# The last four blocks of wo in strips of columns, eight of the strips as two loads of unequal rows

## Chip, cores and metric

The kernel runs on one core of one Trainium2 chip. The metric is the device time of one execution in microseconds (us). Three runs of the kernel before took 773.12 to 773.62 us, median 773.36.

## What is computed

One decode step for a batch of 2 with D = 1024. Branch a is attention over a cache of 32,768 positions (32 query heads, 4 heads of keys and values, head size 128, all fp32); branch b is a small mixer with two layer norms, of which two weights (w1, w2) are not needed at sequence length 1, since every shift by one or two positions leaves only zeros. A sigmoid gate mixes the two:

```python
g = sigmoid((x * gate_w).sum(-1, keepdims=True))
q = (x @ wq)                              # per head
p = softmax(q @ k.T * Dh ** -0.5)
a = concat(p @ v) @ wo                    # wo: 4096 x 1024
b = x + gelu(layernorm(x) @ w3) @ w4      # hs is zero at S = 1
out = g * a + (1 - g) * b
```

The caches and weights are 331 MB, and each byte is used once.

## The kernel before, in words

**Storage.** Two large buffers (`ring`, tiles load0 and load1, 64 KB per partition each) take everything that streams in: wq, w3, the keys and values of eight pairs of batch and head, w4 in between, and most of wo. A third buffer, `tail` (4 * D columns, line 137), is used once, for the last four of the 32 blocks of wo. A block is 128 rows by 1024 columns.

**Order of the transfers.** All big loads are issued by SP through `load` (line 217), in program order, each as soon as the buffer that it writes is free: SP waits for TensorE's mark and then issues. Each load adds 16 to a semaphore once it has fully landed. At the end of the stream wo comes in three pieces into the ring (`weights(wo, STEPS, ...)`, line 272, with 14, 9 and 5 blocks), then four loads into `tail` (lines 273 to 275): blocks 0 and 1 as one load of 128 rows by 2048 columns, then blocks 2 and 3 as 1280, 512 and 256 columns. These four wait for nothing, as `tail` is written only once. They are the last loads of the program; behind them on SP is only the store of `out` (line 640), which has 8 rows.

**What waits for them.** The table `came` (line 215) names the semaphore and the count that says that each of the four has landed: got_x at 32 (16 of them from the load of xg at the start), b_in, pt_in and k1_free. TensorE waits for them at lines 621, 627, 631 and 633.

**The end on TensorE.** After the eighth pair, `weigh` (line 528) multiplies the 28 blocks of wo in the ring into the bank acc, one wait for each of the three pieces (L371 in the profile). Then `block(0..3)` multiplies the four blocks in `tail` into the bank final (L380): blocks 0 and 1 after came[0], then `resumed()` adds what acc holds, then block 2 and a quarter of block 3 after came[1], two quarters after came[2], the last quarter after came[3]. VectorE and ScalarE copy final to out_sb (L638), and SP stores it.

Of the kernel before, what the change touches and what calls it, by code (L numbers as in the profile page):

```python
# [14 lines left out]
P = 128  # L15
B, D, HQ, HKV, SK, DH, F = 2, 1024, 32, 4, 32768, 128, 3584
REP = HQ // HKV
PAIRS = B * HKV
# [6 lines left out]
G = P // C  # L25
# [48 lines left out]
def kernel(  # L74
# [55 lines left out]
    def new(name, *shape, parts=P):  # L130
        return nc.alloc_sbuf_tensor(name, [parts, *shape], F32).ap()
# [5 lines left out]
    tail = new("tail", 4 * D)  # L137
# [57 lines left out]
    def sem(name):  # L195
        cleared.append(nc.alloc_semaphore(name))
        return cleared[-1]
# [8 lines left out]
    got_x = sem("got_x")  # L206
# [5 lines left out]
    step, own_step, to_pe, pt_in, b_in, e_in, x_in, k1_free = (  # L212
        sem(n) for n in ("step", "own_step", "to_pe", "pt_in", "b_in", "e_in", "x_in", "k1_free"))

    came = ((got_x, 32), (b_in, 16), (pt_in, 16), (k1_free, PAIRS + 16))

    def load(dst, src, sem, *marks):
        sp.after(*marks)
        nc.sync.dma_start(dst, src).then_inc(sem, 16)

    def run(src, j):
        return src[PART * j:PART * (j + 1)].rearrange("i (q w) c -> (i q) (w c)", w=PART)
# [9 lines left out]
    def at(name, m=None):  # L232
        if m is None:
            return (pe.sem, 1 + PROLOGUE.index(name))
        return (pe.sem, len(PROLOGUE) + m * len(TURN) + m // 4 * 2 + 1 + TURN.index(name))
# [18 lines left out]
    half = PART * KF // 4  # L254
    STEPS = ((0, 14), (14, 9), (23, 5))

    def weights(src, pieces, *free):
        for (lo, n), landing in zip(pieces, w_in):
            j = lo // half
            piece = slice((lo - j * half) * D, (lo - j * half + n) * D)  # L260
            load(flat[j][:, piece], run(src, j)[:, piece], landing, free[j])
# [8 lines left out]
        for j in range(2):  # L270
            load(flat[j], run(vt[m], j), landed[j], (at("k0", m), (k1_free, m + 1))[j])
    weights(wo, STEPS, at("v0", PAIRS - 1), at("v1", PAIRS - 1))
    load(tail[:, :2 * D], run(wo, 0)[:, half * D:], came[0][0])
    for mark, lo, hi in zip(came[1:], (0, 5, 7), (5, 7, 8)):
        load(tail[:, 2 * D + lo * D // G:2 * D + hi * D // G], run(wo, 1)[:, half * D + lo * D // G:half * D + hi * D // G], mark[0])


# [37 lines left out]
    for i in range(2):  # L315
        own = slice(i * HALF, (i + 1) * HALF)
# [103 lines left out]
    for i in range(2):  # L420
        own = slice(i * HALF, (i + 1) * HALF)
        for s in range(2):
            lo = (2 * s + i) * REP
# [7 lines left out]
    for k2 in range(2):  # L431
        for g in range(G):
            lo = P * (1 - k2)
# [7 lines left out]
    n = KF // G  # L441
# [24 lines left out]
    for i in range(2):  # L466
        for j in range(2):
            own = slice(i * HALF, (i + 1) * HALF)
# [139 lines left out]
    for t, apart, lo, n in ((w_pad, C // B, 0, half), (o_last, 1, half, 2)):  # L608
        for i in range(2):
            own = slice(i * HALF, (i + 1) * HALF)  # L610
# [65 lines left out]
```

## Time and profile before

| | us |
|---|---|
| median of 3 runs | 773.36 (773.12 to 773.62) |
| span of the profiled execution | 771.6 |
| median less span | 1.8 |
| TensorE busy in the span | 436.4 (57%) |
| VectorE busy | 95.2 (12%) |
| ScalarE busy | 60.7 (8%) |
| bytes read from HBM | 331.36 MB, 429 GB/s over the span |
| SP's first issue of a load into tail | 739.90 |
| last instruction, the issue of the store of out | 770.23 |

The times inside the profile are from the start of the span; the 1.8 us between its span and the median of the runs lie outside it. PE is TensorE, PEld its loading of weights, DVE VectorE, ACT ScalarE, SP SyncE; an SPq row is the issue of a transfer and not the transfer itself. The list of DMA issues gives the size of a load and the time from its issue to its landing. In the table of windows each row is a stretch of the span, with the busy time of each engine, the clock that TensorE was granted (PEclk, 1 is full speed), the busy share of the 16 DMA engines and the GB/s that they moved. A "packet" of the DMA rows is one piece of a transfer; a transfer ends with small packets that count up its semaphore.

### The profile page before, as it was taken

What the parts mean: (1) busy time and instruction counts of PE and PEld (TensorE: products, weight loads), DVE (VectorE), ACT (ScalarE), POOL (GpSimd) and SP (SyncE); (2) the same over time, 40 slices, a digit from 0 to 9 for tenths busy, and PEclk for the clock granted to TensorE, in tenths of its full rate; (3) what the DMA queues carried; (4) which work ended last, traced back from release to release, by engine and by line L of the source; (5) the groups of instructions that cost most, each with busy time, mean ns of one, the idle gap of its engine ahead of it and who ended that gap; (6) DMA issues with size and microseconds to landing.
All of it is one profiled execution on the core that took longest, in us unless ns stands there. A gap on an engine that the chain in (4) does not pass through costs nothing. (4 is left out here: it accounts for less than half of the span.)

```text
span 771.6 us, 7439 instructions
## 1 busy us (share of the span) xinstructions
PE 436.4 (57%) x3332; PEld 199.9 (26%) x3332; DVE 95.2 (12%) x269; ACT 60.7 (8%) x144; POOL 3.8 (0%) x13
## 2 busy tenths in 40 slices
PE   0676746564645474546575446454745565646467
PEld 0232413232322232223233213121322232313134
DVE  1110202100210021002100002100210021002110
ACT  0000002000200020002000002000200020002000
POOL 1000000000000000000000000000000000000000
PEclk9977667767787768767766678777777677678788
DMA  9999999999999999999999999999999999999997
GB/s 381 435 436 436 435 436 435 436 436 431 428 431 431 435 435 435 435 435 435 430 428 440 432 435 435 435 435 435 435 435 435 431 431 435 431 435 431 431 424 327
DMA packets 6648, 331.50 MB, mean 430 GB/s; under 512 B 872, under 2 KB 1008, under 8 KB 1264
## 3 DMA queue, kind: packets, MB, share of 16 engines
q1 hardware_dynamic: 6496, 331.36, 99.4%
q8 instruction: 7, 0.11, 0.1%
q10 hardware_dynamic: 144, 0.01, 0.0%
q14 instruction: 1, 0.01, 0.0%
HBM read 331.36 MB, written 0.01 MB: 429 GB/s over the span
## 5 line engine op out<-in xcount | busy, mean ns | idle before, releaser
L488 PE MATMUL sc<-load,q_cur 128*32 128x512 f32 x1024 | 144.1, 722 | 132.3 <-PEq L53 132.3
L514 PE MATMUL pv<-load,pt 128*32 128x512 f32 x1024 | 134.2, 683 | 88.7 <-PEq L53 88.7
L488 PEld LDWEIGHTS sc<-load,q_cur 128*32 128x32 f32 x1024 | 51.2, 130 | 219.2 <-issue 214.8
L514 PEld LDWEIGHTS pv<-load,pt 128*32 128x32 f32 x1024 | 39.2, 124 | 173.9 <-issue 173.9
L505 PE MATMUL sc<-wide,p 128*128 128x128 f32 x256 | 44.5, 347 | 22.8 <-PEq L53 22.8
L571 DVE TENSOR_REDUCE mx<-sc 128x1 f32<-128x512 f32 x32 | 21.4, 689 | 284.8 <-PE sc L488 284.8
L555 ACT ACT_TABLE_LOAD x8 | 10.3, 1283 | 483.0 <-ACTq L53 483.0
L505 PEld LDWEIGHTS sc<-wide,p 128*128 128x128 f32 x256 | 40.1, 184 | 30.0 <-issue 30.0
L371 PE MATMUL acc<-load,w_pad 128*32 128x256 f32 x448 | 34.2, 478 | 18.9 <-PEq L53 18.9
L588 DVE COPY pt<-sc 64x256 f32<-64x256 f32 x64 | 25.9, 414 | 81.4 <-PE sc L505 80.9
L561 ACT COPY pt<-sc 64x256 f32<-64x256 f32 x64 | 23.5, 368 | 85.3 <-PE sc L505 83.0
L593 DVE COPY pv_sb<-pv 128x512 f32<-128x512 f32 x16 | 10.3, 686 | 145.6 <-PE tr L520 145.6
L371 PEld LDWEIGHTS acc<-load,w_pad 128*32 128x32 f32 x448 | 18.6, 137 | 33.6 <-issue 28.7
L524 PE MATMUL tr<-sel,pv_sb 128*128 128x8 f32 x128 | 18.9, 284 | 11.8 <-PEq L53 11.8
L555 ACT ACTIVATE p<-sc,bias 128x512 f32<-128x512 f32 x32 | 21.6, 686 | 0.1
L357 PE MATMUL sc<-load,x_pad 128*32 128x512 f32 x128 | 19.2, 768 | 4.1 <-PEq L53 4.1
L524 PEld LDWEIGHTS tr<-sel,pv_sb 128*128 128x128 f32 x128 | 18.4, 228 | 12.3 <-issue 12.3
L357 PE MATMUL sc<-load,xn_pad 128*32 128x384 f32 (+1 forms) x128 | 15.3, 641 | 7.9 <-PEq L53 7.9
L342 PE MATMUL tr<-xg_sb,perm 128*128 128x16 f32 x4 | 1.0, 372 | 25.2 <-DMA xg_sb<-xg 25.2
L584 DVE COPY p<-p 128x256 f32<-128x256 f32 x32 | 9.4, 294 | 26.7 <-ACT p L555 26.7
L357 PEld LDWEIGHTS sc<-load,xn_pad 128*32 128x32 f32 x128 | 4.8, 130 | 18.4 <-issue 18.4
L357 PEld LDWEIGHTS sc<-load,x_pad 128*32 128x32 f32 x128 | 4.9, 137 | 17.6 <-issue 17.5
(89 smaller groups left out, 96.3 us busy)
## 6 DMA issues: line engine op xcount, KB each, us to landing
load<-w SPq DMA_DIRECT2D x4, 7168.0 KB, 24.9
load<-wo SPq DMA_DIRECT2D x1, 7168.0 KB, 29.0
load<-wo SPq DMA_DIRECT2D x1, 4608.0 KB, 19.3
load<-wo SPq DMA_DIRECT2D x1, 2560.0 KB, 25.0
tail<-wo SPq DMA_DIRECT2D x1, 1024.0 KB, 27.0
tail<-wo SPq DMA_DIRECT2D x1, 640.0 KB, 28.1
load<-kt SPq DMA_DIRECT2D x16, 29.6
load<-vt SPq DMA_DIRECT2D x16, 29.5
```

Source lines behind the costliest of these rows:

```text
L357: last = nc.tensor.matmul(b[C * g:C * g + C, :hi - lo], pad[:, k], t[:, o + lo:o + hi], start=(k == 0), stop=(k == KD - 1))
L371: inst = nc.tensor.matmul(acc[C * g:C * g + C], lhsT, rows[:, g * (D // G):(g + 1) * (D // G)], start=False, stop=last, skip_group_check=True)
L488: last = nc.tensor.matmul(sc[i][C * g:C * g + C], q_cur[:, w, s], ring[j][:, w, o:o + 512], start=(s == 0 and w == 0), stop=(s == 1 and w ...
L505: last = nc.tensor.transpose(sc[k][:, t * P:(t + 1) * P], pair.rearrange("p w q -> p (w q)"), ident)
L514: last = nc.tensor.matmul(pv[C * g:C * g + C], pt[j][w][:, lo:lo + C], ring[j][:, w, o:o + G * DH], start=(j == 0 and w == 0 and t == 0), ...
L524: last = nc.tensor.matmul(tr[1][:, w * REP:(w + 1) * REP], pv_sb[:, s, w].rearrange("p i q -> p (i q)"), sel[:, s], start=(s == 0), stop=( ...
L555: nc.scalar.activation(p[:, i, :, :PART], sc[i].rearrange("p (t q w) -> p t w q", t=NT, w=PART), AF.Exp, bias=bias, scale=scale, accum_out ...
L561: nc.scalar.copy(*halves(1, j, c)).then_inc(pt_in, 1)
L571: last = [nc.vector.reduce_max(out=mx[:, k:k + 1], in_=sc[k], axis=AX.X) for k in ((1, 2) if i == 2 else (i,))][-1]
L584: nc.vector.tensor_copy(p[:, i, :, PART], p[:, i, :, 0]).then_inc(to_pe, 1)
L588: nc.vector.tensor_copy(*halves(0, j, c)).then_inc(pt_in, 1)
L593: last = nc.vector.tensor_copy(pv_sb[:, :, :, i], pv.rearrange("p (s q w) -> p s w q", q=HALF, w=PART))
```

## The change

The first two loads into `tail` become seventeen. Blocks 0 and 1 come as three strips of 64 columns and one of 1856 columns. Each narrow strip is two loads by the new helper `uneven`: the first n partitions, and the 128 - n others, with n = 124, 119 and 125. The first 1280 columns of blocks 2 and 3 come as five strips of 256 columns, each again two loads, with n = 120, 100, 88, 104 and 126. The last two loads (512 and 256 columns) are as before. The counts in `came` follow: got_x now goes to 16 + 7 * 16 and b_in to 10 * 16. The places of the waits, TensorE's work and every other load are the same. All line numbers behind the change move by 12.

```diff
-    came = ((got_x, 32), (b_in, 16), (pt_in, 16), (k1_free, PAIRS + 16))
+    came = ((got_x, 16 + 7 * 16), (b_in, 10 * 16), (pt_in, 16), (k1_free, PAIRS + 16))
...
     weights(wo, STEPS, at("v0", PAIRS - 1), at("v1", PAIRS - 1))
-    load(tail[:, :2 * D], run(wo, 0)[:, half * D:], came[0][0])
-    for mark, lo, hi in zip(came[1:], (0, 5, 7), (5, 7, 8)):
+    def uneven(dst, src, sem, n):
+        for own in (slice(0, n), slice(n, P)):
+            load(dst[own], src[own], sem)
+
+    narrow = 64
+    for i, n in enumerate((124, 119, 125)):
+        cols = slice(i * narrow, (i + 1) * narrow)
+        uneven(tail[:, cols], run(wo, 0)[:, half * D:][:, cols], came[0][0], n)
+    cols = slice(3 * narrow, 2 * D)
+    load(tail[:, cols], run(wo, 0)[:, half * D:][:, cols], came[0][0])
+    for i, n in enumerate((120, 100, 88, 104, 126)):
+        cols = slice(i * D // G, (i + 1) * D // G)
+        uneven(tail[:, 2 * D:][:, cols], run(wo, 1)[:, half * D:][:, cols], came[1][0], n)
+    for mark, lo, hi in zip(came[2:], (5, 7), (7, 8)):
         load(tail[:, 2 * D + lo * D // G:2 * D + hi * D // G], run(wo, 1)[:, half * D + lo * D // G:half * D + hi * D // G], mark[0])
```

On SP, the end of the program before; each row is one load with its rows and columns, first the three pieces of wo, then the four of tail and the store:

```order
L219 DMA load<-wo 128x14336
L219 DMA load<-wo 128x9216
L219 DMA load<-wo 128x5120
L219 DMA tail<-wo 128x2048
L219 DMA tail<-wo 128x1280
L219 DMA tail<-wo 128x512
L219 DMA tail<-wo 128x256
L640 DMA out<-out_sb 8x256
```

Nothing is moved past another load here. On SP in the changed program, from the third piece of wo to the second of the five strips of blocks 2 and 3:

```order
L219 DMA load<-wo 128x5120
L219 DMA tail<-wo 124x64
L219 DMA tail<-wo 4x64
L219 DMA tail<-wo 119x64
L219 DMA tail<-wo 9x64
L219 DMA tail<-wo 125x64
L219 DMA tail<-wo 3x64
L219 DMA tail<-wo 128x1856
L219 DMA tail<-wo 120x256
L219 DMA tail<-wo 8x256
L219 DMA tail<-wo 100x256
L219 DMA tail<-wo 28x256
```

The seventeen loads stand in the place of the two of 2048 and 1280 columns, behind all of the ring's loads; the loads of 512 and 256 columns and the store follow them as before.

## Prediction

> **What bounds the kernel now.** I read the page first, then the chain that ended last, then the end of the timeline, then the transfers of that end. The page says that this is a kernel of transfers:
>
> ```profile
> span 771.6 us, 7439 instructions
> PE 436.4 (57%) x3332; PEld 199.9 (26%) x3332; DVE 95.2 (12%) x269; ACT 60.7 (8%) x144; POOL 3.8 (0%) x13
> ...
> DMA  9999999999999999999999999999999999999997
> ...
> DMA packets 6648, 331.50 MB, mean 430 GB/s; under 512 B 872, under 2 KB 1008, under 8 KB 1264
> ```
>
> The 16 DMA engines are busy in every slice but the last, and TensorE is busy 57% of the time. No byte is saved by the change, so only the last slice can move. What happens there stands in the chain and in the timeline of the end:
>
> ```profile
> 758.40 0.04 issue
> 758.44 9.00 PE acc L371 x112
> 767.44 2.46 PE sc L380 x69
> ```
>
> ```profile
> 767.25 1.06 PE L380 MATMUL sc<-tail,o_wide 128*32 128x128 f32 x32
> ...
> 768.12 0.41 PE L380 MATMUL sc<-so_far,spread 128*32 128x128 f32 x8
> 768.49 0.81 PEld L380 LDWEIGHTS sc<-tail,o_wide 128*32 128x32 f32 x28 [0.23 <-DMA tail<-wo]
> 768.50 1.38 PE L380 MATMUL sc<-tail,o_wide 128*32 128x128 f32 x32
> 769.46 0.14 PEld L380 LDWEIGHTS sc<-tail,o_wide 128*32 128x32 f32 x4 [0.16 <-DMA tail<-wo]
> 769.92 0.28 DVE L638 COPY out_sb<-sc 64x128 f32<-64x128 f32 x1 [1.99 <-PE sc L380]
> 770.23 0.37 SPq L640 DMA_DIRECT2D out<-out_sb  x1
> ```
>
> From 758.44 on TensorE has work to the end. It stands still for the last four blocks of wo (tile tail) only twice, 0.23 us and 0.16 us. So the end has two limits that lie close together: the last strip of tail, and TensorE's own 11.5 us. The first, second and third piece of wo, which start TensorE at 758.44, stand ahead of the changed loads in SP's order and are not touched.
>
> The loads of tail, and the share of the DMA engines that is busy in the last microseconds (the share is the number ahead of the GB/s):
>
> ```profile
> 739.90 1.85 SPq L219 DMA_DIRECT2D tail<-wo  x4
> ...
> tail<-wo SPq DMA_DIRECT2D x1, 1024.0 KB, 27.0
> tail<-wo SPq DMA_DIRECT2D x1, 640.0 KB, 28.1
> ...
> tail<-wo SPq DMA_DIRECT2D x1, 256.0 KB, 28.3
> tail<-wo SPq DMA_DIRECT2D x1, 128.0 KB, 28.1
> ```
>
> ```profile
> 767.00:767.25 0.25, 0.25 (x11) 0.14 (x4) 0.00 (x0) 0.00 (x0) 0.00 (x0) 1.00 0.94 356
> 767.25:767.50 0.25, 0.25 (x16) 0.25 (x12) 0.00 (x0) 0.00 (x0) 0.00 (x0) 1.00 0.66 254
> 767.50:767.75 0.25, 0.25 (x20) 0.25 (x12) 0.25 (x1) 0.00 (x0) 0.00 (x0) 1.00 0.53 213
> ...
> 768.25:768.50 0.25, 0.25 (x13) 0.02 (x4) 0.00 (x0) 0.00 (x0) 0.00 (x0) 1.00 0.44 164
> 768.50:768.75 0.25, 0.25 (x14) 0.25 (x14) 0.00 (x0) 0.00 (x0) 0.00 (x0) 1.00 0.41 143
> 768.75:769.00 0.25, 0.25 (x18) 0.25 (x10) 0.00 (x0) 0.00 (x0) 0.00 (x0) 1.00 0.17 57
> ```
>
> This is the view that matters. The engines do not finish together. About half of them run dry between 767.25 and 767.5, the share then stands near one half for a whole microsecond, and the other half ends between 768.5 and 769.0. Each load is done only when its slowest engine is, so half of the engines set the end and half idle for about 1.5 us. I see a likely source in the queues between 45 and 435 us, which hold all the packets of program code in the span:
>
> ```profile
> DMA packets 2968, 169.21 MB, mean 434 GB/s; under 512 B 320, under 2 KB 320, under 8 KB 320
> ...
> q8 instruction: 7, 0.11, 0.1%
> q14 instruction: 1, 0.01, 0.0%
> ```
>
> Eight code packets (those of q8 have 16 KB each) went through the same engines, and eight engines are late. An engine that fetched code once would stay late, since its queue is never empty. Which engines these are the trace does not name.
>
> **The change part by part.** First, what a row costs an engine. The four loads were issued about 0.47 us apart from 739.90 on (1.85 us in all, the last one 0.43 of it), so they landed at 766.9, 768.5, 769.15 and 769.4. The second brings eight rows of 5 KB to each engine, and took 1.57 us, 39 ns per KB; the third, eight rows of 2 KB, 0.68 us, 42 ns per KB. I take 40 ns per KB, so 40 ns for a row of 1 KB. A row of 256 bytes is not in the trace. The nearest are the 96-byte rows of xg on the other queue:
>
> ```profile
> q10 hardware_dynamic: 48, 0.00, 0.3%
> ```
>
> In the window from 20 to 30 us, 0.3% of 16 engines over 10 us is 0.48 us for 48 packets, 10 ns each. So a 256-byte row costs at least 10 ns (which is also a quarter of 40) and at most the 40 ns of 1 KB; I take 15, near the 96-byte row and on the line between the two.
>
> [...]
>
> Second, which engine gets which rows. A transfer of 128 rows closes with one small packet per engine. The page counts 872 packets under 512 bytes, and that is 45 loads with 16 each, 144 of xg, and 8 more: the store of out, whose 8 rows went to 8 engines:
>
> ```profile
> DMA packets 16, 0.01 MB, mean 27 GB/s; under 512 B 8, under 2 KB 16, under 8 KB 16
> ```
>
> (the window of that store, 771.0 to 771.3: eight rows of 1 KB and eight closings). Both shapes go out in equal shares. I take it that every load does: its rows go in equal shares to the largest number of engines, up to 16, that divides them, and to the same first engines each time. Then 124 rows are 31 on each of four engines, 119 are 17 on seven, 125 are 25 on five, 88 are 8 on eleven.
>
> [...] The store's 8 closings agree; unequal rows no run has shown yet.
>
> Now the sum for an engine's share of tail. Before: 8 rows each of 8, 5, 2 and 1 KB, 128 KB, 5.12 us. After, each engine keeps 8 rows of the wide strip (1856 columns, 7.25 KB, 2.32 us) and the last two loads (0.96 us), 3.28 us. The three narrow strips add 76 rows of 256 bytes to the first three engines (31+1+17+1+25+1), 75 to the fourth, 43 to the fifth, 18 to the sixth and seventh, one or none to the others. The five strips of 1 KB add 52 or 53 rows to the first eight engines, 51 to the ninth and tenth, then 37, 29, 27, 19, 8 and none. So:
>
> The first four: 3.28 + 76 x 15 ns + 52.5 x 40 ns = 6.52 us, 1.40 more than before, and with 15 more closing packets at 10 ns about 1.5 us more. The fifth: about 1.0 more. The sixth and seventh: 0.6. The eighth to tenth: 0.3 to 0.4. The last six: 0.4, 0.7, 0.8, 1.1, 1.5 and 1.8 us less. The change is a steep tilt of work from the last engines to the first.
>
> SP issues 15 more loads, at 0.47 us each 7 us, from 739.9 to about 749; the first of these rows is not reached before 764, so this lies beside 15 us of queued pieces of wo, and costs nothing. If that cover were gone, 7 us would show. Behind these issues on SP only the store of out is queued, at 770.23. TensorE's waits stay four, at the same places, with larger counts; blocks 0 and 1 need the narrow strips and the wide one, which for a first engine come 0.97 us later than the 8 KB rows did (3.46 against 2.56, and closings). They landed at 766.9, TensorE took them up at 767.25, and an early engine hides the rest in its 1.5 us.
>
> The gain is bounded by TensorE: without its two waits it ends 0.39 us earlier, no more, however well the engines are levelled. The loss has no such floor: whatever the last engine loses comes straight to the end.
>
> **My forecast: the heavy engines are early ones.** The first four then end at 767.25 to 767.5 plus 1.5, 768.75 to 769.0, just where the late ones end today (769.0). The eighth to tenth, if late, end 0.3 later. So 0 to +0.3 us; I take +0.1. The span of 771.6 becomes 771.7; the median of the runs shown, 773.36, has 1.8 us around that span which I leave as they are: 773.5. The reason to take the first engines for early ones: if code packets walk round the engines in order, the late ones are a block, and a block of eight out of sixteen clears the first four in 5 of 16 places, against 1 in 26 for scattered ones. And no code came in the first 45 us, so what TensorE ran until then was loaded ahead of the span; if that loading began at the first engine, the eight of the span fell on later ones. That is an argument from order, and thin.
>
> **The rivals.** One: a heavy engine is a late one. It then ends at 768.5 to 769.0 plus 1.5, 770.0 to 770.5, that is 1.05 to 1.55 us behind today's end; TensorE waits for it at the second wait of the tail, and the whole goes to the end. Taking 1.3, the time is 774.7. It decides as soon as one of the first four engines ends later than about 767.5 today. For it: half of the engines are late and nothing names them. Against it: only the order of the code packets.
>
> Two: the levelling works. If the late engines are just the relieved six or so and a 256-byte row costs 10 ns, the heavy ones end at 768.5, and TensorE's two waits shrink or go: 0.39 us less, 773.0. For it: the measured 1.5 us of idle half. Against it: the last six are relieved more than they are late, and eight engines are late, not six.
>
> Three: the change does not do what it says, and rows are spread evenly over 16 engines whatever their count. Then each engine pays 24 rows of 256 bytes at 15 in place of 10 ns, 0.12 us, and some 15 closings, 0.15 us: 773.6.
>
> Four: the small rows are dear. At 40 ns the first engines pay 1.9 us more, and even early ones end 1.9 us behind today: 775.3.
>
> **How the numbers follow.** A measurement of this kernel can tell about 0.2% from no change, 1.55 us. Chances: forecast 0.42; a heavy engine late 0.30; levelling works 0.13; even spread 0.08; dear rows 0.05; 0.02 for a gain that I don't see. Of the late case about 0.4 lies above 1.55 us with a 256-byte row at the upper end, 0.12; with the dear rows 0.17 slower. Faster than 0.2% has no mechanism, since TensorE allows 0.39 us: 0.03. The rest, 0.80, is the same. The range goes from the levelled case, 772.9, to the upper part of the late case, 775.0; what is left out is the dear rows and the tail of the late case.
>
> **What would show it.** In the changed profile: packets under 512 bytes up by 384 rows and by the closings of the new loads, fewer than 16 for each uneven one; the landings of tail against 766.9 and 769.4; the busy share between 767 and 770 (a step at one half that shrinks if levelled, a thin share of a few engines up to 770.5 if a heavy engine is late); TensorE's waits for tail (0.39 us in all now). I am wrong if the time moves by over 1.55 us, if TensorE before 767 changes, or if the share of busy engines shows the tail of a few engines that my forecast denies.

## The result, and the profile after

The changed kernel takes 776.81 us (median of 4 runs, 776.62 to 777.08) against 773.34 for the kernel before: 3.47 us more, a ratio of 1.0047 (95% interval 1.0035 to 1.0058). The forecast was 773.5 in a range of 772.9 to 775.0, so it is wrong, and on the slow side of every case in the prediction. The span of the profiled execution went from 771.6 to 775.1 us.

The page after, with its count of packets:

```profile
span 775.1 us, 7454 instructions
...
DMA packets 7669, 331.50 MB, mean 428 GB/s; under 512 B 1381, under 2 KB 2157, under 8 KB 2413
```

Packets under 512 bytes went from 872 to 1381, 509 more. 384 of these are the rows of 256 bytes, and 125 are closings. If each load runs on the largest number of engines up to 16 that divides its rows, the seventeen loads have 4+4, 7+9, 5+3, 16, 15+8, 10+14, 11+10, 13+12 and 14+2, in all 157 closings in place of 32, which is the 125 that the page has. So a load runs on as many engines as the prediction took, and the change does what it says. That these are the same first engines each time, the page doesn't show.

The end on TensorE and SP's issues, from the timeline of the changed kernel:

```profile
768.84 1.08 PE L392 MATMUL sc<-tail,o_wide 128*32 128x128 f32 x32 [1.62 <-DMA tail<-wo]
769.71 0.43 PE L392 MATMUL sc<-so_far,spread 128*32 128x128 f32 x8
...
771.41 1.94 PE L392 MATMUL sc<-tail,o_wide 128*32 128x128 f32 x32 [1.27 <-DMA tail<-wo]
...
773.45 0.28 DVE L650 COPY out_sb<-sc 64x128 f32<-64x128 f32 x1 [5.73 <-PE sc L392]
```

```profile
740.18 25.68 SPq L219 DMA_DIRECT2D tail<-wo  x19
```

TensorE now waits 1.62 us for blocks 0 and 1, where it did not wait, and 1.27 us for blocks 2 and 3. The last 32 products start at 771.41, which was 768.50: 2.91 us later. They then take 1.94 us in place of 1.38. Together 3.47 us, and the copy starts 3.53 us later (773.45 against 769.92). So two things carry the loss: tail lands later, and TensorE runs its last products slowly. For the second there is the granted clock in the windows of the same stretch (the number after the engines' busy times, ahead of the DMA share and the GB/s):

```profile
767.00:768.00 1.00, 0.23 (x6) 0.00 (x0) 0.42 (x1) 0.00 (x0) 0.00 (x0) 1.00 1.10 238
768.00:769.00 1.00, 0.16 (x8) 0.19 (x12) 0.00 (x0) 0.00 (x0) 0.00 (x0) 1.00 1.04 216
769.00:770.00 1.00, 1.00 (x40) 0.87 (x32) 0.00 (x0) 0.00 (x0) 0.00 (x0) 1.00 0.79 212
770.00:771.00 1.00, 0.14 (x7) 0.00 (x0) 0.00 (x0) 0.00 (x0) 0.00 (x0) 1.00 0.45 152
...
772.00:773.00 1.00, 1.00 (x28) 0.82 (x20) 0.00 (x0) 0.00 (x0) 0.00 (x0) 0.50 0.00 0
```

The clock is 0.50 in the last row. In the kernel before it was 1.00 to the end:

```profile
769.00:770.00 1.00, 0.88 (x24) 0.38 (x14) 0.08 (x1) 0.08 (x1) 0.00 (x0) 1.00 0.00 0
```

And the first two rows of the changed kernel show what no case of the prediction had: the DMA engines are fully busy (share 1.10 and 1.04) and move 238 and 216 GB/s. Compare the kernel before, two microseconds earlier, in its own loads of tail:

```profile
765.00:766.00 1.00, 1.00 (x28) 0.60 (x23) 0.00 (x0) 0.00 (x0) 0.00 (x0) 1.00 1.02 420
766.00:767.00 1.00, 1.00 (x24) 0.64 (x20) 0.00 (x0) 0.00 (x0) 0.00 (x0) 1.00 1.01 400
```

A share of one bought 400 to 420 GB/s there. By the trace's packet records a row of 1 KB of the loads took 67 ns on average in the changed kernel and 46 ns before. It isn't mainly that a few engines have too much to do. The trace records a landing of the last load (256 columns) for each of its sixteen engines. Before, the last of the sixteen came at 769.42; in the changed kernel fifteen come later than that. Their mean moved by 2.19 us (768.53 to 770.72), the last one by 2.80 (to 772.22).

### The profile page after: what moved, and what is told of

Its sections match the earlier page's. It is cut to its first block, busy times and chain, and to the rows that moved or that the text cites. A ratio compares the mean times of both kernels' runs of the same rounds, so it can differ in the third digit from the quotient of the medians.

```text
span 775.1 us, 7454 instructions
## 1 busy us (share of the span) xinstructions
PE 440.6 (57%) x3332; PEld 200.7 (26%) x3332; DVE 95.1 (12%) x269; ACT 60.6 (8%) x144; POOL 3.8 (0%) x13
## 2 busy tenths in 40 slices
DMA packets 7669, 331.50 MB, mean 428 GB/s; under 512 B 1381, under 2 KB 2157, under 8 KB 2413
## 5 line engine op out<-in xcount | busy, mean ns | idle before, releaser
L500 PE MATMUL sc<-load,q_cur 128*32 128x512 f32 x1024 | 147.6, 737 | 129.2 <-PEq L53 129.2
```

The costliest lines, as they stand in the source:

```text
L500: last = nc.tensor.matmul(sc[i][C * g:C * g + C], q_cur[:, w, s], ring[j][:, w, o:o + 512], start=(s == 0 and w == 0), stop=(s == 1 and w ...
```

## The experiments

Four theories, guesses of the author's, were tried. **Tilt**: the first engines have too much work, and one of them is late. **Meeting**: rows of loads that have not 128 rows are written by other engines than usual, meet other rows on the way to the same partitions, and slow each other. **Rows**: the small rows and the closings themselves are dear. **Issue**: SP's issues stall (25.68 us in place of 1.85) and come too late. Times are set against the kernel before on the same chip. In the diffs the counts in `came`, which follow the number of loads, are left out, and so is the semaphore `extra`, on which GpSimd waits at the end of the program.

**e1: the strips without the unevenness.**

```diff
-        for own in (slice(0, n), slice(n, P)):
+        for own in (slice(0, n), slice(n, P)) if n else (slice(0, P),):
...
-    for i, n in enumerate((124, 119, 125)):
+    for i, n in enumerate((None, None, None)):
...
-    for i, n in enumerate((120, 100, 88, 104, 126)):
+    for i, n in enumerate((None, None, None, None, None)):
```

> The same ten strips of columns, each as one load of 128 rows: no uneven shares, every engine has 8 rows of each strip. Tilt theory (the first engines have too much): +0.1 to +0.3 us over before, the price of the smaller rows alone. Meeting theory (rows of one load that two engines bring to the same group of partitions slow each other): the same, +0.1 to +0.3, 1 KB rows at 46 ns as in before, not 65. Row theory (small rows and closings are what costs): +1.5 us or more, with 1 KB rows above 60 ns. Issue theory (SP's issues stall and come too late): SP issues fewer packets, so part of the 25.7 us stays and with it at least 1 us.

Measured: 773.63 against 773.12, +0.51 us (ratio 1.0007, 0.9997 to 1.0016). The 1 KB rows took 48 ns. In its timeline, SP's issues and TensorE's last products:

```profile
741.62 20.94 SPq L219 DMA_DIRECT2D tail<-wo  x11
```

```profile
769.14 1.40 PE L392 MATMUL sc<-tail,o_wide 128*32 128x128 f32 x32 [0.26 <-DMA tail<-wo]
```

SP's issues stall for 20.9 us here too, and the time hardly moves. Small rows and their closings cost half a microsecond, somewhat more than expected. The row theory explains a seventh of the loss; a stall of this size alone does not bring the loss about.

**e2: uneven in nothing but the number of rows.** Each of the eight strips is two loads of 64 rows, so every engine has 4 rows of each: its page has 1496 packets under 512 bytes, the 872 of before, 384 rows and 16 closings for each of the 15 loads more.

```diff
-    for i, n in enumerate((124, 119, 125)):
+    for i, n in enumerate((64, 64, 64)):
...
-    for i, n in enumerate((120, 100, 88, 104, 126)):
+    for i, n in enumerate((64, 64, 64, 64, 64)):
```

> All eight strips as two loads of 64 rows, 17 loads as in the changed kernel: every engine has 4 rows of each load, so 8 of each strip and no tilt. Tilt theory: +0.2 to +0.5 us, only rows and closings. Meeting theory: the 16 engines write into half of the partitions at a time, so rows of the strips take up to twice as long: 640 KB in 1 KB rows, 40 rows an engine with up to 46 ns more, +1.5 to +2.2 us. Issue theory: 17 loads but fewer packets on the first engine, +1 us or less.

Measured: 775.80 against 773.12, +2.68 us (1.0035, 1.0021 to 1.0050), with 1 KB rows at 66 ns. Nothing is tilted here, and most of the loss is there. The meeting theory had this, if a little low. SP's issues stall here too (24.46 us); whether that is the loss, e5 shows. Its windows show the same signs as those of the changed kernel, a full share at a low rate, and the slow clock at the end:

```profile
767.00:768.00 1.00, 0.46 (x11) 0.00 (x0) 0.42 (x1) 0.00 (x0) 0.00 (x0) 1.00 1.04 226
768.00:769.00 1.00, 0.08 (x4) 0.11 (x8) 0.00 (x0) 0.00 (x0) 0.00 (x0) 1.00 1.11 258
...
772.00:773.00 1.00, 0.99 (x20) 0.51 (x14) 0.00 (x0) 0.00 (x0) 0.00 (x0) 0.50 0.00 0
```

**e3 and e4: one half of the change each.** e3 keeps the uneven narrow strips and loads the 1280 columns of blocks 2 and 3 as before; e4 keeps the five uneven strips and loads blocks 0 and 1 as before.

```diff
 # e3
-    for i, n in enumerate((120, 100, 88, 104, 126)):
...
+    load(tail[:, 2 * D:][:, :5 * D // G], run(wo, 1)[:, half * D:][:, :5 * D // G], came[1][0])
 # e4
-    for i, n in enumerate((124, 119, 125)):
...
+    load(tail[:, :2 * D], run(wo, 0)[:, half * D:], came[0][0])
```

> Only the three narrow strips are uneven; the 1280 columns of blocks 2 and 3 are one load as before. Tilt theory: the first four engines have 52 rows of 256 bytes more, 0.9 to 1.1 us, and if one of them is late this shows in full: +0.9 to +1.2. Meeting theory: only 96 KB go uneven, +0.2 to +0.5. Issue theory: the first engines' packets are the same 75 that stalled SP, so its stall stays, and the time is +1 us or more only if the stall matters.

> Only the five strips of 256 columns are uneven; blocks 0 and 1 are one load as before. Tilt theory: the first eight engines have 12 or 13 rows of 1 KB more, 0.55 us, so +0.5 to +0.8 if one of them is late and 0 if none. Meeting theory: 640 KB go uneven, 1 KB rows at 60 ns and more, +1.5 to +2.5 us. Issue theory: no narrow rows ahead, SP stalls less, below +0.5 us.

Measured: e3 773.91, +0.79 us (1.0011, 1.0001 to 1.0020); e4 775.05, +1.93 us (1.0025, 1.0015 to 1.0035), each against 773.12. For e3 the tilt theory's number is the nearer one; for e4 only the meeting theory's fits. Together they are 2.72 of 3.47 us, if two halves measured apart may be added. The last products take 1.38 us in e3 and 1.39 in e4:

```profile
770.63 1.39 PE L387 MATMUL sc<-tail,o_wide 128*32 128x128 f32 x32 [0.42 <-DMA tail<-wo]
```

(e4), so the 0.56 us of slow clock is in neither; with it the sum is 3.28.

**e5: the smallest edit that meets.** Before, with one load made two. Nothing small, nothing uneven, no stall.

```diff
-    for mark, lo, hi in zip(came[1:], (0, 5, 7), (5, 7, 8)):
+    for lo in range(0, P, 64):
+        own = slice(lo, lo + 64)
+        load(tail[own, 2 * D:][:, :5 * D // G], run(wo, 1)[own, half * D:][:, :5 * D // G], came[1][0])
+    for mark, lo, hi in zip(came[2:], (5, 7), (7, 8)):
```

> Before, with the load of 1280 columns alone made two loads of 64 rows: 4 rows of 5 KB an engine each, no tilt, no small rows, one load more. Meeting theory (16 engines write into half of the partitions at a time): 5 KB rows well above 199 ns, up to 390, +0.7 to +1.6 us. Tilt, row and issue theories: nothing that they price is changed, 0 to +0.1 us.

Measured: 776.46 against 773.15, +3.31 us (1.0044, 1.0027 to 1.0061). Its windows, and SP's issues:

```profile
765.00:766.00 1.00, 1.00 (x27) 0.73 (x20) 0.00 (x0) 0.00 (x0) 0.00 (x0) 1.00 1.07 238
766.00:767.00 1.00, 0.97 (x20) 0.37 (x12) 0.00 (x0) 0.00 (x0) 0.00 (x0) 1.00 1.01 221
767.00:768.00 1.00, 0.00 (x0) 0.00 (x0) 0.42 (x1) 0.00 (x0) 0.00 (x0) 1.00 0.93 191
```

```profile
741.56 2.73 SPq L219 DMA_DIRECT2D tail<-wo  x5
```

One load in two halves costs as much as the whole change. From 765 to 767 the engines are busy and move 238 and 221 GB/s, a little over half of the 420 and 400 of before; 5 KB rows take 339 ns on average, not 199. The loss was larger than expected because the loads around it slow too (8 KB rows 378 ns, not 313) and TensorE's last products again take 1.94 us. The tilt, row and issue theories have nothing to say here. Why two loads of 64 rows run at this rate, no run shows.

**e6: the same load as eight of 16 rows.**

```diff
 # e6, against e5
-    for lo in range(0, P, 64):
-        own = slice(lo, lo + 64)
+    for lo in range(0, P, 16):
+        own = slice(lo, lo + 16)
```

> The same load as eight loads of 16 neighbouring rows, one row of 5 KB an engine each: no tilt, no small rows, seven loads more. [...] Tilt, row and issue theories: 7 more closings and issues, +0.1 to +0.2 us.

Measured: 775.79 against 773.15, +2.64 us (1.0036, 1.0024 to 1.0049), 5 KB rows at 327 ns. The tilt, row and issue theories have 0.1 to 0.2 us for it, so this too is meeting. But sixteen neighbouring rows are no worse than sixty-four (327 ns against 339 in e5): eight loads in place of two slow the rows no further.

**e7 and e8: the same work on as many engines, in other partitions.** Five extra loads of 4 rows of 8 KB, into an unused end of the ring (work that the reference doesn't need). The rows of a load lie four partitions apart in e7 and next to each other in e8. A load of 4 rows lands on four engines (e12), so if all five go to the same four, each of these heavy engines has five rows more, 1.56 us at the 313 ns that a row of 8 KB took before. That they are the first four is the author's assumption.

```diff
+    for first in (0, 1, 2, 3, 32):
+        own = slice(first, first + 13, 4)
+        load(flat[0][own, 14 * D:], run(wo, 0)[own, :2 * D], extra)
 # e8, against e7
-    for first in (0, 1, 2, 3, 32):
-        own = slice(first, first + 13, 4)
+    for first in (0, 4, 8, 12, 32):
+        own = slice(first, first + 4)
```

> [...] If a heavy engine is a late one: +1.3 to +1.6 us. If all four are early: 0 to +0.2 us. The meeting theory expects no longer rows, 312 ns for 8 KB.

> As the run before, but the 4 rows of each extra load are neighbours (0 to 3 and the like): the same bytes on the same engines. Tilt theory: the same time as the run before. [...]

Measured: e7 774.00, +0.85 us (1.0011, 1.0001 to 1.0020); e8 774.79, +1.64 us (1.0021, 1.0011 to 1.0030), both against 773.15. Windows of e7 and of e8 while the extra rows come:

```profile
765.00:766.00 1.00, 1.00 (x25) 0.70 (x21) 0.00 (x0) 0.00 (x0) 0.00 (x0) 1.00 1.02 425
```

```profile
765.00:766.00 1.00, 0.82 (x16) 0.65 (x20) 0.00 (x0) 0.00 (x0) 0.00 (x0) 1.00 0.95 311
```

With rows four apart the rate stays at 425 GB/s, and 8 KB rows take 313 ns, as before. With neighbouring rows the rate is 311, and 8 KB rows take 395 ns on average, up to 815. The same bytes in the same number of loads and rows, where the tilt theory expected the same time: meeting. No run of e7 (773.75 to 774.38) took as long as the fastest of e8 (774.54). And e7 is the tilt by itself: 1.56 us of work on four engines cost 0.85, between the prediction's two cases. In its landings of the first load of tail, the eight early engines have become five; three have moved back by the 1.56 us, and one late engine now comes 2.99 us behind the first, where in before the last came 1.78 us behind. So five loads went to the same four engines, and of these three are early and one is late.

**e9, e13 and e14: written or read?** e9 is e5 with its rows read from one unbroken stretch of wo (other values). e13 is e7 with e8's places of reading, e14 is e8 with e7's; the extra rows are needed by nothing.

```diff
 # e9, against e5
+    packed = run(wo, 1)[:10].rearrange("p c -> (p c)").rearrange("(p c) -> p c", c=5 * D // G)
...
-        load(tail[own, 2 * D:][:, :5 * D // G], run(wo, 1)[own, half * D:][:, :5 * D // G], came[1][0])
+        load(tail[own, 2 * D:][:, :5 * D // G], packed[own], came[1][0])
 # e13, against e7
-        own = slice(first, first + 13, 4)
+        own, near = slice(first, first + 13, 4), slice(first, first + 4)
-        load(flat[0][own, 14 * D:], run(wo, 0)[own, :2 * D], extra)
+        load(flat[0][own, 14 * D:], run(wo, 0)[near, :2 * D], extra)
 # e14, against e8
-        own = slice(first, first + 4)
+        own, far = slice(first, first + 4), slice(first, first + 13, 4)
-        load(flat[0][own, 14 * D:], run(wo, 0)[own, :2 * D], extra)
+        load(flat[0][own, 14 * D:], run(wo, 0)[far, :2 * D], extra)
```

> As e5 (1280 columns as two loads of 64 rows), but the rows come from one unbroken stretch of wo instead of rows 64 KB apart (other values, the same bytes to the same places). If what slows the rows is where they are written: as slow as e5, 5 KB rows around 340 ns, +2.5 to +3.5 us. If it is where they are read: near before, rows near 200 ns, 0 to +0.5 us.

> As e7 (extra rows written to partitions 0, 4, 8, 12 and the like by the first four engines), but read from four neighbouring rows of wo, as in e8. If the place of writing decides: as e7, +0.8 to +0.9 us, 8 KB rows at 313 ns. If the place of reading decides: as e8, +1.6 us.

> As e8 (extra rows written to neighbouring partitions), but read from rows of wo that lie four apart, as in e7. If the place of writing decides: as e8, +1.5 to +1.8 us, 8 KB rows near 395 ns on average. If the place of reading decides: as e7, +0.8 to +0.9 us.

Measured: e9 776.43 against 773.27, +3.16 us (1.0037, 1.0024 to 1.0050), 5 KB rows at 338 ns, as e5. e13 773.92 against 773.12, +0.80 us (1.0011, 1.0001 to 1.0020), 8 KB rows at 313 ns, as e7. e14 774.68, +1.56 us (1.0021, 1.0011 to 1.0030), 404 ns, as e8. The first microseconds of the extra rows, in e13 and in e14:

```profile
764.00:765.00 1.00, 0.66 (x16) 0.34 (x12) 0.00 (x0) 0.00 (x0) 0.00 (x0) 1.00 1.00 417
765.00:766.00 1.00, 1.00 (x27) 0.72 (x20) 0.00 (x0) 0.00 (x0) 0.00 (x0) 1.00 0.98 407
```

```profile
764.00:765.00 1.00, 0.00 (x0) 0.00 (x0) 0.00 (x0) 0.00 (x0) 0.00 (x0) 1.00 1.02 240
765.00:766.00 1.00, 0.85 (x16) 0.66 (x20) 0.00 (x0) 0.00 (x0) 0.00 (x0) 1.00 0.90 273
```

417 and 407 GB/s, against 240 and 273. The time follows the place of writing; a change of the place of reading shows in none of the three.

**e10 and e11: sixteen rows next to each other or seven apart.** Four extra loads of 16 rows of 8 KB, one row of each on every engine: both pages have 936 packets under 512 bytes, 64 more than before, 16 closings a load.

```diff
+    for first in (0, 16, 32, 48):
+        own = slice(first, first + 16)
+        load(flat[0][own, 14 * D:], run(wo, 0)[own, :2 * D], extra)
 # e11, against e10
-    for first in (0, 16, 32, 48):
-        own = slice(first, first + 16)
+    for first in (0, 1, 2, 3):
+        own = slice(first, first + 106, 7)
```

> Before, with four extra loads of 16 neighbouring rows of 8 KB ahead of tail into the unused end of the ring: one row of each on every engine, 1.25 us of work for each, no tilt. Meeting theory: rows that lie next to each other slow each other, +2.2 to +4.5 us, with rows far above 312 ns. Without meeting: +1.2 to +1.4 us, the bytes alone.

> As e10, but the 16 rows of each extra load lie 7 partitions apart, so that they reach far more of the groups of partitions. Meeting theory: clearly less than e10, +1.2 to +2.2 us. Without meeting, or if it depends only on the number of rows of a load: the same as e10.

Measured: e10 778.32, +5.05 us (1.0064, 1.0046 to 1.0082); e11 777.48, +4.21 us (1.0057, 1.0039 to 1.0075), both against 773.27. 8 KB rows took 527 and 464 ns on average. Both lie above what was expected. The order is as expected, but the intervals overlap, and in e10's trace TensorE's first 32 products of tail took 1.94 us where e11's took 1.08, so the clock has a part in the difference. The rows that lie apart are far from free: 4.21 us for 1.25 us of work. Rows that spread over the partitions may still meet the loads before and behind them; that is not shown, nor that partitions form groups, which the expectation takes for granted, and these two runs alone don't tell the place of writing from the mere number of rows of a load. e7 and e8 do.

**e12: where the late engines sit.** Before, with five small loads behind the last one.

```diff
+    for i, (k, probe) in enumerate(zip((1, 2, 4, 8, 12), probes)):
+        load(flat[0][:k, 14 * D + i * 64:][:, :64], run(wo, 0)[:k, i * 64:(i + 1) * 64], probe)
```

> Before, with five small extra loads behind the last one, of 1, 2, 4, 8 and 12 rows of 256 bytes, which go to the first 1, 2, 4, 8 and 12 engines if a load is shared so: when each lands says where the late engines sit. From e7 one of the first four is late, so the load of 4 rows should land with the late half (1.4 us or more behind the first landing), and the load of 1 or 2 rows early if that engine is the third or fourth. The time is 0 to +0.1 us over before.

Measured in one run: 773.18 us against 773.27. In the trace each engine with rows of a load adds its own step to the load's semaphore, so that a load of 4 rows shows four landings: the load of 1 row at 767.75; of 2 rows at 767.93 and 768.01; of 4 rows at 768.10, 768.19, 768.22 and 768.87; of 8 rows five up to 768.39 and three from 769.04; of 12 rows seven up to 768.57 and five from 769.23 on. If these loads go to the same first engines each time, the author's assumption, which no run shows, then the first two engines are early, one of the third and fourth is late, two of the next four, two of the next four, and three of the last four; and the late ones are scattered and not a block.

**e15: nearly even shares in loads of the same kind.** As e4, but each strip as 120 and 8 rows.

```diff
-    for i, n in enumerate((120, 100, 88, 104, 126)):
+    for i, n in enumerate((120, 120, 120, 120, 120)):
```

> As e4 (only the five strips of 256 columns are uneven), but each split 120 and 8: the first eight engines get 9 rows of each strip, seven get 8, the last none, so that the tilt on the heavy ones is 5 rows of 1 KB, 0.2 us, against 12 or 13 rows in e4. Tilt theory: +0.4 to +0.7 us, strips included. Meeting theory: the strips still go out in other places than a load of 128 rows, so nearly what e4 took, +1.3 to +2.1 us.

Measured: 774.84 against 773.12, +1.72 us (1.0024, 1.0014 to 1.0034), of e4's 1.93. The heavy engines have 5 rows too many here and 12 or 13 in e4. The difference of 0.2 us between the two lies within the noise: their intervals nearly coincide. So most of e4's loss is there with little tilt.

## Why the prediction was wrong, point by point

**The step that failed** is the price of a row in "the sum for an engine's share": 40 ns per KB, taken from loads of 128 rows and used for loads of 120, 100, 88 and so on, as if it belonged to the engine alone. It depends on the partitions that a load writes: extra rows of 8 KB run at 313 ns where the four of a load lie four partitions apart (e7, e13), and take 395 and 404 ns where they lie next to each other (e8, e14). How the place slows them, no run shows. In the changed kernel a 1 KB row took 67 ns and not 46. For the 40 such rows of an engine that is 0.8 us, and the 7.25 KB rows behind and between them, 354 ns on average against 298 in e1, add eight times 56 ns, 0.45 us; eight 2 KB rows at 118 ns in place of 85 add 0.26 us. This falls on the engines as a whole: the landings of the last load moved by 2.19 us on average, where the prediction's own shares come to about 0.2 us a piece on average and relieve six engines by 0.4 to 1.8 us.

**The sharing of the rows**, taken from loads of 128 and of 8 rows, was right in the number of engines, by the 125 closings; that they are always the same first engines, no run shows, and e7 shows for its five loads only that they went to the same four. **The tilt** was there and is real, but small in this result: the last landing moved 0.61 us more than the mean of the sixteen (2.80 against 2.19), e15 is not clearly faster than e4, and e7 puts 0.85 us on 1.56 us of clean work for four engines. **That the heavy engines are early** was wrong for one of four (e7, e12), and the argument for a block from the order of the code packets fell with e12, if its loads go to the first engines; the eight code packets and the eight late engines stay a match, not a shown cause. Rival one was therefore right about its engine; its price for it, 1.3 us, stands against the 0.85 of e7, and neither reaches 3.47. The match of code packets and late engines holds in time too. In the trace of before, the number of engines that land a ring load over 0.6 us behind the first rises one by one, each time in the loads behind a code packet. It is none at 42 us, six from 172 on (the sixth packet came at 159.9), still six at 402, seven at 419 (packet at 412.4) and eight from 438 on (packet at 430.5).

**The small rows** cost 0.51 us with their closings (e1), where the even spread was worked out at 0.27. By the packet records a 256-byte row took 18 ns in e1 and 22 in the changed kernel, near the 15 taken and far from the 40 of rival four. **SP's issues** were put at 7 us for the fifteen more and took 25.68 for all nineteen. The profile's own chain of the changed kernel runs through them:

```profile
SPq 3%; PE 1%; DMA 1%; issue 0%; DVE 0%
```

Yet "costs nothing" held for e1, whose 20.94 us came with half a microsecond, and e5 lost 3.31 us with 2.73 us of issues. Nor did the engines run dry behind the stall: from 763 to 769 their busy share was 0.92 to 1.10 in every microsecond. Whether the later end of the stall in the changed kernel adds a little was not separated.

**TensorE's bound on a gain**, 0.39 us, was never reached. **The loss "comes straight to the end"** fell short: the end moved 3.53 us for 2.91 us of later landing, since TensorE's last products met a granted clock of 0.50. That is a term of 0.56 us that the prediction did not have. It is not shown that every run of the changed kernel had it: the last products of e4 and e6, from 770.63 and 771.05, had the full clock and took 1.39 and 1.15 us, and e2's profiled run, with the slow clock, took 776.26 us where its median is 775.80. Why the clock fell is open.

The sum by the runs: 0.79 (e3) and 1.93 (e4), each with its part of the small rows, and 0.56 for the clock, 3.28 of 3.47 us. The parts come from different kernels, the clock's from one trace, so the sum is a tally and not a proof. That the shares in the changed kernel are slowed by the same meeting as in e5 and e8 rests on the same signs, a full busy share at a low rate (216 to 238 GB/s, 221 to 238 in e5, 311 in e8, against 400 to 420). What stays open is the dose: why 16 neighbouring rows were no worse than 64 (e6), and why rows seven apart helped so little (e11).

## What to carry to other kernels

The price of a transfer's row is not a property of its size: in this stream of loads of 128 partitions, one load made two of 64 rows brought the rate from 400 to 420 GB/s down to 221 to 238 while the engines read as busy (e5), and loads of 4 rows that lay four partitions apart left it at 425 (e7), so look at the GB/s beside the busy share. To shift work between DMA engines by the number of rows cost 3.47 us here, several times the 0.39 that the levelling could have given. Before pricing an edit that changes the shape of a transfer, look for a row of that shape in the trace, and where there is none, keep a case in which it halves the rate.

## What the runs showed of the hardware

- A load of 640 KB in two halves of 64 rows in place of one of 128 ran at 221 to 238 GB/s where 400 to 420 were usual, and cost 3.31 us (e5); read from elsewhere it cost 3.16 (e9).
- The same 160 KB in five loads of 4 rows cost 0.85 us where the rows of a load lay four partitions apart and 1.64 us where they were neighbours (e7, e8).
- SP's issue of 11 loads took 20.94 us with nothing to wait for by the program (e1), and of 5 loads 2.73 us (e5).
- The DMA engines of this kernel land up to 1.8 us apart in each load of before, eight early and eight late through the last 300 us, and the number of late ones rises by one behind each of the eight code packets of the span (a match in time, not a shown cause).
